# Relu² attention with an expert layer behind it: the high part of the routed rows made by ScalarE, and z split on one half of the partitions

## The chip, the cores and the metric

The kernel runs on one core of a Trainium2 chip. The metric is the device time of one execution in microseconds (us); the time shown for a kernel is the median of its runs. The five engines are TensorE (PE, with its weight loads shown apart as PEld), VectorE (DVE), ScalarE (ACT), GpSimd (POOL) and SyncE (SP), which here only issues DMAs.

## The reference

```python
def _attn_ref(u, v, z):                      # u, v: 8 x 2496 x 256, z: 8 x 2496 x 64
    scores = (1.0 / S) * np.matmul(z, z.transpose(0, 2, 1))
    attn = np.maximum(scores, 0.0) ** 2
    return u * np.matmul(attn, v)

def _moe_ref(x, expert_emb, tau, w1, w2):    # x: 19968 x 256, 8 experts, F = 1024
    xn, en = x / (norm(x) + 1e-6), expert_emb / (norm(expert_emb) + 1e-6)
    logits = xn @ en.T / tau
    expert_idx = np.argmax(logits, axis=1)
    gate_w = softmax(logits)[np.arange(N), expert_idx]
    for e in range(E):
        mask = expert_idx == e
        out[mask] = gate_w[mask, None] * (np.maximum(x[mask] @ w1[e], 0.0) @ w2[e])
```

The attention's output, 8 × 2496 rows, is the x of the expert layer. All is float32.

## The kernel before, in words

Every float32 operand of a large matmul is split into two float16 parts, a high part (the rounded value, scaled by a power of two) and a low part (the scaled value minus the high part), and a product is made of three or two float16 matmuls. So most splits are a pair of instructions: one that writes the high part and one that reads it back and subtracts.

**Attention.** Each of the 8 batches is worked in five groups g of 512 queries (the last has 448) by 20 tiles s of 128 keys, 100 steps per batch. `scores` (lines 257, 258) makes scores of one step in PSUM, ScalarE makes the relu and the square (`a`, lines 260, 261), and `parts` (lines 281, 282) makes the high and low part of it on VectorE (`hl`, or `joint` for the halved tiles on the diagonal). As the scores are symmetric, only steps with s // 4 >= g, the own steps, are computed; the others use tiles that DMA transposes have turned (`tt`, line 288). Scores run three own steps ahead. `values` (lines 320, 322, 324) multiplies by v into `acc`.

**z.** For the scores a batch needs two tiles of 128 partitions by 2560 columns: `z1` has the high part on partitions 0 to 63 and the low part on 64 to 127, `z2` the other way round. `z_load` (line 172) loads z twice, on both halves of the partitions, 256 columns at a time, into one of three buffers `zt`, and `z_split` (lines 183 to 186) makes the four parts, high ones on ScalarE (183, 184), low ones on VectorE (185, 186). The ten pieces of the next batch are split at steps 68, 70, ... 86 of the batch before; its first scores are made at step 97.

**v.** `v_load` (line 192) and `v_split` (229 on ScalarE, 230 on VectorE) run some steps ahead in the same way, in buffers `vt` and `vv`.

**Routing.** When a group ends, its 512 rows are routed by a queue of small functions, of which each step of the next group takes one: `gate_x` (352, multiplies acc by u into `xt`), `turn` (358, 359, matmuls that transpose and make the logits), `take` (369, ScalarE copies them to `x`), `square` (365, ScalarE), `root` and `scale` (608 to 622 and 378 to 387 on VectorE, which make the scale `up` and the logits), `top` (406 to 418, up to the one-hot `ob`), `exps` (424), four `split`s (395 the high, 396 the low part of 128 rows, into `row`), `gates`, `rank` (441, matmuls on `ob` that count), `place`, and `scatters` (465, GpSimd writes the rows to memory, sorted by expert).

**Weights of the experts** are split in the same time: `maxes` (504) and `scales` (510, 512), and four parts each (555 ScalarE, 556 VectorE, into `wo`), of which every second is followed by a 1 MB store to `wsd` (559).

**Expert layer.** From 1328 us on, PE runs the experts' matmuls (lines 869 to 895); the matmuls are nearly alone there.

**Order.** The order of PE's instructions is that of the program (a manual schedule). That of VectorE, ScalarE, GpSimd and SP is chosen by a scheduler at build time; each engine then takes its instructions strictly in that order. Dependencies are kept by regions of a tile.

Of the kernel before, what the change touches and what calls it, by code (L numbers as in the profile page):

```python
# [13 lines left out]
AF = mybir.ActivationFunctionType  # L14
ALU = mybir.AluOpType
# [4 lines left out]
P = 128  # L20
# [11 lines left out]
def ceil_div(a, b):  # L32
    return -(-a // b)
# [11 lines left out]
def relu2_attention_then_moe(ctx, tc, zT, uT, v, emb, tau, w1, w2, ident, tri, iota_e, out):  # L45
    nc = tc.nc
    B, D, S = uT.shape
    DQ = zT.shape[1] // 2
# [6 lines left out]
    SP = NST * P  # L55
# [34 lines left out]
    Zs = {}  # L90
# [9 lines left out]
    def scan_load(b, what, i, eng=None):  # L100

        t = wk.tile([P, SCAN], F32, name="scan", tag="scan", bufs=2)
        if what == "z":
            src = zT[b, i * (DQ // ZSCANS):(i + 1) * (DQ // ZSCANS), :]
        else:
            src = v[b, i * (SP // VSCANS):(i + 1) * (SP // VSCANS), :]
        (eng or nc.sync).dma_start(t, src.rearrange("a c -> (a c)").rearrange("(p w) -> p w", p=P))
        scan[b, what, i] = t

    def scan_max(b, what, i):  # L110
        if i == 0:
            n = ZSCANS if what == "z" else VSCANS if b else NV0
            scan[b, what] = sml.tile([P, n], F32, name="smx" + what)
        nc.vector.tensor_reduce(scan[b, what][:, i:i + 1], scan.pop((b, what, i)), axis=AX.X, op=ALU.max,
                                apply_absolute_value=True)
# [47 lines left out]
    def z_tiles(b):  # L163
        Zs[b] = (zpool.tile([P, SP], F16, name="z1", tag="z1"),
                 zpool.tile([P, SP], F16, name="z2", tag="z2"))

    ZC = 256

    def z_load(b, c0):
        zt = zpool.tile([P, ZC], F32, name="zt", tag="zt", bufs=3)  # L170
        c1 = min(c0 + ZC, SP)
        nc.sync.dma_start(zt[:, :c1 - c0], zT[b, :, c0:c1])
        zraw[b, c0] = zt

    def z_split(b, c0):
        zt = zraw.pop((b, c0))
        w = min(ZC, SP - c0)
        c1 = c0 + w
        z1, z2 = Zs[b]
        c = slice(c0, c1)  # L180
        lo, hi = slice(0, DQ), slice(DQ, P)
        k = scan[b, "cz"]
        nc.scalar.activation(z1[lo, c], zt[lo, :w], AF.Copy, scale=k[lo])
        nc.scalar.activation(z2[hi, c], zt[hi, :w], AF.Copy, scale=k[hi])
        nc.vector.scalar_tensor_tensor(z2[lo, c], zt[lo, :w], k[lo], z1[lo, c], op0=ALU.mult, op1=ALU.subtract)
        nc.vector.scalar_tensor_tensor(z1[hi, c], zt[hi, :w], k[hi], z2[hi, c], op0=ALU.mult, op1=ALU.subtract)  # L186

    vraw = {}

# [142 lines left out]
    def route(b, g, acc, ut):  # L332
# [8 lines left out]
        xk = x.rearrange("p j (k c) -> p j k c", k=2)[:, :, :, 0:P]  # L341
# [49 lines left out]
        def split(j):  # L391
            up = loc["up"][:, j:j + 1]
            hi = row16[:, j, 0:D].rearrange("p (k c) -> p k c", k=2)
            lo = row16[:, j, D:2 * D].rearrange("p (k c) -> p k c", k=2)
            nc.vector.tensor_scalar_mul(hi, xk[:, j], up)
            nc.vector.scalar_tensor_tensor(lo, xk[:, j], up, hi, op0=ALU.mult, op1=ALU.subtract)

        def splits(j0):
            def f():
                for j in range(j0, min(j0 + 2, nj)):  # L400
                    split(j)
            return f
# [173 lines left out]
    ZN = ceil_div(SP, ZC)  # L576
    for k in range(2):
        z_load(0, k * ZC)
    for i in range(NV0):
        v_first(i)  # L580
    z_load(0, 2 * ZC)
    for what, i in SCANS[:ZSCANS]:
        scan_max(0, what, i)
    for f in scale_pieces(0, "z"):
        f()
    for k in range(2):
        z_split(0, k * ZC)
# [5 lines left out]
    for i in range(NV0):  # L593
        scan_max(0, "v", i)
        if i == NV0 - 2:
            halves[direct[0]] = parts(*direct[0], probs.pop(direct[0]))
    z_load(0, 3 * ZC)
    for f in scale_pieces(0, "v"):
        f()
# [339 lines left out]
    def ahead(b):  # L939

        todo = []
        at = min(NST + 4, NB // 4)
        for i, what in enumerate(SCANS):
            todo.append((at + 2 * i, False, lambda w=what: scan_load(b + 1, *w)))
            todo.append((at + 2 * i + 4, False, lambda w=what: scan_max(b + 1, *w)))
        at += 2 * len(SCANS) + 4
        for k, what in enumerate("zv"):
            for j, f in enumerate(scale_pieces(b + 1, what)):
                todo.append((at + 8 * k + 4 * j, True, f))
        at = max(at + 20, (NG - 2) * NST // 2) if NG > 2 else at + 20  # L950
        gap = max(1, (NB - early - at) // ZN)
        todo.append((0, False, lambda: z_tiles(b + 1)))
        for k in range(ZN):
            todo.append((max(0, at + (k - 3) * gap), False, lambda k=k: z_load(b + 1, k * ZC)))
            todo.append((at + k * gap, False, lambda k=k: z_split(b + 1, k * ZC)))
        return sorted(todo, key=lambda x: x[0])

    todo = []
    nd = 0
    for i, (b, g, q, s) in enumerate(steps):  # L960
        own = s // GT >= g
        if i % 2 == 0 and zk < ZN:
            if zk + 2 < ZN:
                z_load(0, (zk + 2) * ZC)
            z_split(0, zk * ZC)
            zk += 1
# [3 lines left out]
        if q == 0:  # L970
            accs[b, g] = [psA.tile([P, 512], F32, name=f"acc{k}", tag=f"a{2 * ((b * NG + g) % 2) + k}") for k in range(2)]
            nx = (b, g + 1) if g + 1 < NG else (b + 1, 0)
            if nx[0] < B:
                uts[nx] = u_load(*nx)
            if g == 0 and b + 1 < B:
                todo = ahead(b)
# [34 lines left out]
        if b + 1 < B:  # L1011
            if (g == NG - 2 and q >= NST - early) or (NG > 1 and g == NG - 1) or NG == 1:
                k = q - (NST - early) if g == NG - 2 else q + early
# [128 lines left out]
```

## Time and profile before

| | |
|---|---|
| median of 3 runs | 2179.89 us (2178.35 to 2180.82) |
| profiled execution | 2175.33 us, span 2173.6 us |
| granted TensorE clock in it | 0.999 |
| PE busy | 2127.6 us, 98% |
| DVE busy | 1370.5 us, 63% |
| ACT busy | 1063.2 us, 49% |
| POOL busy | 337.9 us, 16% |
| DMA | 313.85 MB, 144 GB/s on average |

Busy times are shares of the span, an average over stages: DVE and ACT work mostly in the first 1300 us, PE throughout. In rows of the timeline the columns are the start, the duration, engine, line, operation, `out<-in`, shapes, count, and in brackets the idle time of the engine before it with what ended it. In rows of groups they are count, busy time, mean ns of one, and the idle time before. In rows of waits they are the total, the number and the longest.

### The profile page before, as it was taken

What the parts mean: (1) busy time and instruction counts of PE and PEld (TensorE: products, weight loads), DVE (VectorE), ACT (ScalarE), POOL (GpSimd) and SP (SyncE); (2) the same over time, 40 slices, a digit from 0 to 9 for tenths busy, and PEclk for the clock granted to TensorE, in tenths of its full rate; (3) what the DMA queues carried; (4) which work ended last, traced back from release to release, by engine and by line L of the source; (5) the groups of instructions that cost most, each with busy time, mean ns of one, the idle gap of its engine ahead of it and who ended that gap; (6) DMA issues with size and microseconds to landing.
All of it is one profiled execution on the core that took longest, in us unless ns stands there. A gap on an engine that the chain in (4) does not pass through costs nothing. (4 is left out here: it accounts for less than half of the span.)

```text
span 2173.6 us, 41442 instructions
## 1 busy us (share of the span) xinstructions
PE 2127.6 (98%) x14634; PEld 1406.9 (65%) x14634; DVE 1370.5 (63%) x4051; ACT 1063.2 (49%) x2193; POOL 337.9 (16%) x428
## 2 busy tenths in 40 slices
PE   6999999999999999999999999999999999999999
PEld 2445445545455545445545447888888888888898
DVE  7788788778788888788778664433333333333333
ACT  7567567667658667567667552222222222222211
POOL 0011111111111111111111111221111211111111
PEclk9999999999999999999999999999999999999999
DMA  7958767876867958767856852434323332246484
GB/s 199 210 106 223 168 159 186 183 180 148 204 156 179 224 112 221 170 156 186 186 129 136 174 95 91 136 72 96 86 53 89 91 94 52 50 122 191 128 219 116
DMA packets 554964, 313.85 MB, mean 144 GB/s; under 512 B 474741, under 2 KB 517118, under 8 KB 546560
## 3 DMA queue, kind: packets, MB, share of 16 engines
q1 hardware_dynamic: 539280, 269.53, 54.2%
q0 software_dynamic: 15184, 41.24, 5.9%
q8 instruction: 117, 1.92, 0.4%
q14 instruction: 95, 0.78, 0.1%
q10 hardware_dynamic: 288, 0.39, 0.1%
HBM read 277.53 MB, written 59.60 MB: 155 GB/s over the span
## 5 line engine op out<-in xcount | busy, mean ns | idle before, releaser
L260 ACT ACTIVATE a<-sc 128x512 f32<-128x512 f32 (+1 forms) x480 | 269.4, 561 | 168.2 <-PE sc L258 115.5
L261 ACT ACTIVATE a<-a 128x512 f32<-128x512 f32 (+1 forms) x480 | 286.8, 597 | 13.0
L324 PEld LDWEIGHTS <-vv 128*128 128x128 f16 x1600 | 156.7, 98 | 185.9 <-issue 8.2
L320 PEld LDWEIGHTS <-vv 128*128 128x128 f16 x1600 | 156.5, 98 | 159.8 <-ACT vv L229 1.1
L900 POOL DMA_INDIRECT out_dram<-ot,me x159 | 154.7, 973 | 653.5 <-DVE ot L899 629.3
L322 PEld LDWEIGHTS <-vv 128*128 128x128 f16 x1520 | 148.8, 98 | 163.1 <-issue 11.8
L895 PE MATMUL po<-w,hl 128*128 128x256 f16 x928 | 252.9, 273 | 0.0
L893 PE MATMUL po<-w,hh 128*128 128x256 f16 x928 | 252.9, 273 | 0.0
L894 PE MATMUL po<-w,hh 128*128 128x256 f16 x928 | 252.9, 273 | 0.0
L320 PE MATMUL acc<-tt,vv 128*128 128x512 f16 (+1 forms) x640 | 235.9, 369 | 0.0
L322 PE MATMUL acc<-tt,vv 128*128 128x512 f16 (+1 forms) x640 | 235.8, 368 | 0.0
L465 POOL DMA_INDIRECT xs<-row,dsti x160 | 166.0, 1038 | 391.0 <-DMA xs<-row,dsti 336.0
L899 DVE TENSOR_SCALAR ot<-po,me,w 128x256 f32<-128x256 f32 x116 | 58.3, 540 | 220.3 <-PE po L895 219.0
L324 PE MATMUL acc<-tt,vv 128*128 128x512 f16 (+1 forms) x640 | 183.5, 368 | 0.0
L257 PE MATMUL sc<-z 128*128 128x512 f16 (+1 forms) x480 | 175.7, 366 | 3.7 <-DVE z L186 3.1
L258 PE MATMUL sc<-z,z 128*128 128x512 f16 (+1 forms) x480 | 175.7, 366 | 0.0
L894 PEld LDWEIGHTS <-hh 128*128 128x128 f16 x1272 | 124.5, 98 | 15.1 <-issue 0.9
L895 PEld LDWEIGHTS <-hl 128*128 128x128 f16 x1272 | 124.5, 98 | 14.4
L893 PEld LDWEIGHTS <-hh 128*128 128x128 f16 x1272 | 124.5, 98 | 14.3
L369 ACT COPY x<-pt 128x264 f32<-128x264 f32 x160 | 59.6, 372 | 129.3 <-PE pt L359 126.5
L893 PE MATMUL po<-wb,hh 128*128 128x256 f16 x344 | 93.8, 273 | 0.8 <-DMA wb<-wsd 0.8
L895 PE MATMUL po<-wb,hl 128*128 128x256 f16 x344 | 93.8, 273 | 0.0
(3881 smaller groups left out, 4980.1 us busy)
## 6 DMA issues: line engine op xcount, KB each, us to landing
w<-wsd SPq DMA_DIRECT2D x64, 1026.0 KB
wa<-wsd SPq DMA_DIRECT2D x46, 1024.0 KB
w<-wsd SPq DMA_DIRECT2D x42, 1024.0 KB
wb<-wsd SPq DMA_DIRECT2D x24, 1026.0 KB
vt<-in_v_dram SPq DMA_DIRECT2D x140, 128.0 KB
scan<-in_v_dram SPq DMA_DIRECT2D x56, 320.0 KB
ut<-in_uT_dram SPq DMA_DIRECT2D x32, 512.0 KB
wr<-in_w_dram SPq DMA_DIRECT2D x16, 1024.0 KB
```

The costliest lines, as they stand in the source:

```text
L257: nc.tensor.matmul(sc[:, :n], z1[:, ss], z1[:, t0:t0 + n], start=True, stop=False)
L258: nc.tensor.matmul(sc[:, :n], z1[:, ss], z2[:, t0:t0 + n], start=False, stop=True)
L260: state["at"] = nc.scalar.activation(a[:, :n], sc[:, :n], AF.Relu, scale=2.0 ** -SHIFT).ins
L261: nc.scalar.activation(a[:, :n], a[:, :n], AF.Square)
L320: nc.tensor.matmul(o, va, ph, start=first, stop=False)
L322: nc.tensor.matmul(o, vb, ph, start=False, stop=False)
L324: nc.tensor.matmul(o, vb if last else va, pl, start=False, stop=ends)
L465: put = nc.gpsimd.indirect_dma_start(xs[:, :], bass.IndirectOffsetOnAxis(ap=loc["dsti"][:m, j:j + 1], axis=0), row[:m, j, :], None)
L893: nc.tensor.matmul(o, hh[:, f, t], wh, start=(f == 0), stop=False)
L894: nc.tensor.matmul(o, hh[:, f, t], wl, start=False, stop=False)
L895: nc.tensor.matmul(o, hl[:, f, t], wh, start=False, stop=(f == NF - 1))
L900: put = nc.gpsimd.indirect_dma_start(out, bass.IndirectOffsetOnAxis(ap=me.bitcast(U32)[:, j, 1:2], axis=0), ot[:, j, :], None, bounds_chec ...
```

## The change

There are two parts. In `split` the high part of a routed row is made by ScalarE's Copy with scale `up` in place of VectorE's multiplication; the low part stays on VectorE and reads it. And for every batch but the first, z is loaded on 64 partitions only and split there (two instructions for a piece in place of four); after pieces 5 and 9 a new function `z_copy` copies the columns that are ready to the other 64 partitions by two DMAs each, the low part of `z2` to `z1` and the high part of `z1` to `z2`. Lines behind the change are moved on by 9 (260 to 269, 281 to 290, 365 to 374, 369 to 378, 395 to 404, 396 to 405, 418 to 427, 441 to 450, 555 to 564, 608 to 617).

```diff
     def z_load(b, c0):
         ...
-        nc.sync.dma_start(zt[:, :c1 - c0], zT[b, :, c0:c1])
+        m = P if b == 0 else DQ
+        nc.sync.dma_start(zt[:m, :c1 - c0], zT[b, :m, c0:c1])
     def z_split(b, c0):
         ...
         nc.scalar.activation(z1[lo, c], zt[lo, :w], AF.Copy, scale=k[lo])
-        nc.scalar.activation(z2[hi, c], zt[hi, :w], AF.Copy, scale=k[hi])
+        if b == 0:
+            nc.scalar.activation(z2[hi, c], zt[hi, :w], AF.Copy, scale=k[hi])
         nc.vector.scalar_tensor_tensor(z2[lo, c], zt[lo, :w], k[lo], z1[lo, c], op0=ALU.mult, op1=ALU.subtract)
-        nc.vector.scalar_tensor_tensor(z1[hi, c], zt[hi, :w], k[hi], z2[hi, c], op0=ALU.mult, op1=ALU.subtract)
+        if b == 0:
+            nc.vector.scalar_tensor_tensor(z1[hi, c], zt[hi, :w], k[hi], z2[hi, c], op0=ALU.mult, op1=ALU.subtract)
+
+    def z_copy(b, c0, c1):
+        z1, z2 = Zs[b]
+        c = slice(c0, c1)
+        nc.sync.dma_start(z1[DQ:P, c], z2[0:DQ, c])
+        nc.sync.dma_start(z2[DQ:P, c], z1[0:DQ, c])
     ...
         def split(j):
             ...
-            nc.vector.tensor_scalar_mul(hi, xk[:, j], up)
+            nc.scalar.activation(hi, xk[:, j], AF.Copy, scale=up)
             nc.vector.scalar_tensor_tensor(lo, xk[:, j], up, hi, op0=ALU.mult, op1=ALU.subtract)
     ...
         for k in range(ZN):
             todo.append((max(0, at + (k - 3) * gap), False, lambda k=k: z_load(b + 1, k * ZC)))
             todo.append((at + k * gap, False, lambda k=k: z_split(b + 1, k * ZC)))
+            if k in (ZN // 2, ZN - 1):
+                c0, c1 = (0, (k + 1) * ZC) if k == ZN // 2 else ((ZN // 2 + 1) * ZC, SP)
+                todo.append((at + k * gap, False, lambda c0=c0, c1=c1: z_copy(b + 1, c0, c1)))
```

The order of PE's instructions is the same before and after. That of the others shifts. On VectorE, at the beginning of the routing of batch 1's group 0 (`xn2c` to `up` belong to root and scale, `xt2` and `xy` to the square root, `hl` to own steps), before:

```order
L381 TENSOR_SCALAR up_2973<-h23_2971 128x4
L383 TENSOR_SCALAR dn_2975<-h23_2971 128x4
L615 TENSOR_TENSOR xt_2934<-xy_2932 128x4
L395 TENSOR_SCALAR row_2779<-x_2776,up_2973 128x256
L617 SCALAR_TENSOR_TENSOR xt2_2936<-xt_2934,xn2c_2928 128x4
L395 TENSOR_SCALAR row_2779<-x_2776,up_2973 128x256
L281 CAST hl__2908<-a_2876 128x4x128
L114 TENSOR_REDUCE smxz_2918<-scan_2835 128x1
L282 TENSOR_TENSOR hl__2908<-a_2876,hl__2908 128x4x128
```

and after:

```order
L390 TENSOR_SCALAR up_2957<-h23_2955 128x4
L392 TENSOR_SCALAR dn_2959<-h23_2955 128x4
L624 TENSOR_TENSOR xt_2918<-xy_2916 128x4
L626 SCALAR_TENSOR_TENSOR xt2_2920<-xt_2918,xn2c_2912 128x4
L628 SCALAR_TENSOR_TENSOR xy_2922<-xt2_2920,xy_2916 128x4
L443 TENSOR_SCALAR row_3201<-iot_222 128x4
L624 TENSOR_TENSOR xt_2924<-xy_2922 128x4
L290 CAST hl__2892<-a_2860 128x4x128
L114 TENSOR_REDUCE smxz_2902<-scan_2819 128x1
L291 TENSOR_TENSOR hl__2892<-a_2860,hl__2892 128x4x128
```

The two high parts ahead of the cast are gone, and pieces of the square root have moved up.

On ScalarE, at the routing of batch 0's group 3, beside splits of v and the last parts of an expert's weights (`pt` is what the matmuls of `turn` write), before:

```order
L369 COPY x_1952<-pt_2049 128x264
L365 ACTIVATE sq_2085,n2_1954<-x_1952 128x256
L229 ACTIVATE vv_2069<-vt_1999,scv_1561 128x256
L369 COPY x_1952<-pt_2065 128x264
L365 ACTIVATE sq_2098,n2_1954<-x_1952 128x256
L555 ACTIVATE wo_2180<-wr2_818,wup_1649 128x512
L229 ACTIVATE vv_2087<-vt_2023,scv_1561 128x256
L555 ACTIVATE wo_2180<-wr2_818,wup_1649 128x512
```

and after:

```order
L378 COPY x_1942<-pt_2033 128x264
L374 ACTIVATE sq_2069,n2_1944<-x_1942 128x256
L564 ACTIVATE wo_2164<-wr2_818,wup_1649 128x512
L238 ACTIVATE vv_2053<-vt_1987,scv_1561 128x256
L378 COPY x_1942<-pt_2049 128x264
L564 ACTIVATE wo_2164<-wr2_818,wup_1649 128x512
L374 ACTIVATE sq_2082,n2_1944<-x_1942 128x256
L238 ACTIVATE vv_2071<-vt_2009,scv_1561 128x256
L564 ACTIVATE wo_2164<-wr2_818,wup_1649 128x512
L238 ACTIVATE vv_2084<-vt_2023,scv_1561 128x256
L404 ACTIVATE row_1945<-x_1942,up_2134 128x256 x2
```

Two parts of the weights now stand ahead of the last square, and the high parts of the rows follow behind it.

On SP, near the end of batch 1 (`zt` and `vt` are loads for batch 2, `ut` for the next group, `wr2` a weight load), before:

```order
L559 DMA wsd_73<-wo_3818 128x4096
L172 DMA zt_3997<-in_zT_dram 128x256
L496 DMA wr2_4162<-in_w2_dram 128x8x256
L329 DMA ut_4042<-in_uT_dram 128x2x512
L172 DMA zt_4053<-in_zT_dram 128x256
L192 DMA vt_4097<-in_v_dram 128x256
```

and after:

```order
L568 DMA wsd_73<-wo_3798 128x4096
L194 DMA z1_2338<-z2_2339 64x1536
L195 DMA z2_2339<-z1_2338 64x1536
L173 DMA zt_3971<-in_zT_dram 64x256
L338 DMA ut_4016<-in_uT_dram 128x2x512
L173 DMA zt_4025<-in_zT_dram 64x256
L201 DMA vt_4067<-in_v_dram 128x256
```

The first pair of copies stands ahead of the last loads of zt; the second pair comes eight loads later.

## The prediction

> **What bounds the kernel.** I read the totals of the page first, then the time by stages, then what TensorE waits for, and last the timeline around each of these waits.
>
> ```profile
> PE 2127.6 (98%) x14634; PEld 1406.9 (65%) x14634; DVE 1370.5 (63%) x4051; ACT 1063.2 (49%) x2193; POOL 337.9 (16%) x428
> ```
>
> TensorE (PE) is busy for 2127.6 of 2173.6 us. A change that takes no matmul away can win at most the other 46 us, and only those parts that the touched engines cause. The stages, as window and its length, then PE, weight loads, DVE, ACT and POOL busy, the granted clock, the DMA share and GB/s:
>
> ```profile
> 60.00:1220.00 1160.00, 1145.13 (x5871) 581.98 (x5870) 949.23 (x3118) 779.96 (x1674) 160.53 (x230) 1.00 0.73 172
> 1290.00:2173.00 883.00, 876.00 (x8276) 774.83 (x8274) 332.51 (x659) 206.97 (x363) 167.50 (x175) 1.00 0.42 105
> ```
>
> Attention and routing fill the first window: PE is idle there for 1160 − 1145.13 = 14.9 us, DVE is busy 82% and ACT 67% of the time. In the second window DVE works 38% and ACT 23%; what the change does after 1290 us (17 of the 160 high parts) lies beside matmuls and is costed at nothing; at worst, if all 17 stood on the path, it would be 17 × 0.4 = 7 us. The waits of PE from 60 to 1220 us (total, times, longest):
>
> ```profile
> PE pm L441 <- DVE ob L418: 4.7, 3, 1.7
> PE pt L358 <- DVE xt L352: 2.3, 2, 1.5
> PE acc L320 <- DVE hl__5470 L281: 1.9, 1, 1.9
> PE pm L512 <- DVE mx L510: 1.3, 2, 1.0
> PE acc L320 <- DVE hl__7183 L281: 0.9, 1, 0.9
> PE acc L320 <- DVE hl__11329 L281: 0.4, 1, 0.4
> PE acc L320 <- DVE hl__3015 L281: 0.4, 1, 0.4
> PE acc L324 <- DVE hl__5470 L282: 0.4, 1, 0.4
> PE acc L324 <- DVE hl__13784 L282: 0.4, 1, 0.4
> PE acc L320 <- DVE hl__13784 L281: 0.3, 1, 0.3
> PE acc L324 <- DVE hl__7075 L282: 0.3, 1, 0.3
> PE acc L324 <- DVE hl__7148 L282: 0.3, 1, 0.3
> PE acc L320 <- DVE hl__7272 L281: 0.2, 1, 0.2
> ```
>
> Their sum is 13.8 us, and every releaser is DVE. So the change works on the right engine, but the pot is 13.8 us, 0.6% of the time.
>
> **The change, part by part.** The prices, by shape:
>
> ```profile
> L396 DVE SCALAR_TENSOR_TENSOR row<-x,up,row 128x256 f16<-128x256 f32 x160 | 76.0, 476 | 0.0
> L395 DVE TENSOR_SCALAR row<-x,up 128x256 f16<-128x256 f32 x160 | 54.9, 347 | 0.0
> L186 DVE SCALAR_TENSOR_TENSOR z<-zt,scz,z 64x256 f16<-64x256 f32 x80 | 38.8, 485 | 3.2
> L184 ACT ACTIVATE z<-zt,scz 64x256 f16<-64x256 f32 x80 | 40.2, 503 | 1.7
> L229 ACT ACTIVATE vv<-vt,scv 128x256 f16<-128x256 f32 x133 | 63.0, 500 | 16.1 <-PE acc L324 8.2 <-DVE scv L142 4.3 <-DMA vt<-in_v_dram 2.6
> ...
> 180.06 1.69 ACT L229 ACTIVATE vv<-vt,scv 128x256 f16<-128x256 f32 x4
> 441.00 0.34 DVE L395 TENSOR_SCALAR row<-x,up 128x256 f16<-128x256 f32 x1
> 441.26 0.15 DVE L617 SCALAR_TENSOR_TENSOR xt<-xt,xn2c 128x4 f32<-128x4 f32 x1
> ```
>
> Instructions of one engine overlap a little, so what one takes from its neighbours is the distance between starts: on DVE a high part takes 441.26 − 441.00 = 0.26 us. On ACT its nearest row is the split of v, the same shape and function: four in 1.69 us, (1.69 − 0.50) / 3 = 0.40 us each. DVE is freed of 160 × 0.26 = 41.6 us and of 70 halves of z at 0.485, 34 us. ACT gains 160 × 0.40 = 64 us and loses 70 × 0.50 = 35 us, in net +29 us, to 70% of the first window. All this lies beside PE; it counts only at the waits above, so I go through them.
>
> *Routing beside own steps* (first excerpt of the order). In batch 1's routing of group 0 the wait is this:
>
> ```profile
> 248.97 0.41 DVE L281 CAST hl__3015<-a 128x512 f16<-128x512 f32 x1
> 249.43 0.38 PE L320 MATMUL acc<-hl__3015,vv 128*128 128x512 f16 x1 [0.44 <-DVE hl__3015 L281]
> ```
>
> DVE runs its queue back to back here, and four high parts stood ahead in the same route, 4 × 0.26 = 1.05 us. That is more than the 0.44 us of the wait, so it goes. The same holds for hl__11329 (0.4) and for the two waits on mx behind them (1.3): −2.1 us. For hl__7075, 7148, 7183 and 7272 (1.7 together, one place) a saving of 1.05 is all that is ahead: −1.05. Next late there is the same cast, by the 0.65 left.
>
> *The three waits of rank on ob* (4.7): in each the four high parts stand on DVE between root and ob, so I take −1.05 of each, −3.1. Against it stands that ACT is now longer just there (second excerpt of the order):
>
> ```profile
> 169.94 0.34 SPq L559 DMA_DIRECT2D wsd<-wo  x1
> 174.45 0.17 DVE L608 TENSOR_SCALAR xn2c<-n 128x4 f32<-128x4 f32 x1
> 176.79 0.72 ACT L555 ACTIVATE wo<-wr,wup 128x512 f16<-128x512 f32 x1 [2.38 <-DMA wsd<-wo]
> ```
>
> The weight split (L555, after L564) waits until the store of the piece before has landed, 176.79. It now stands ahead of the last take and square, on which root (174.45) rests. Taken at these times root would be 176.79 + 0.72 + 0.4 + 0.6 − 174.45 = up to 4 us later; but the store too may be earlier, since wo's pieces have less of ACT and DVE before them. Bounds for the three together: −4.7 to +6 (two of the three places have this order). I stay at −3.1, since behind root there are fewer splits of v than before.
>
> *hl__5470* (1.9 + 0.4) stands behind high parts too, the one at 441.00 above:
>
> ```profile
> 443.74 0.41 DVE L281 CAST hl__5470<-a 128x512 f16<-128x512 f32 x1
> ```
>
> But there three of the four now lie on ACT ahead of the next relu, so that its operand comes later by about what DVE gains: 0, bounds −1.05 and +1. *xt* (2.3) is not behind any high part in this route, *hl__13784* (0.7) neither: 0, with −0.7 as the gain if freed DVE time reaches them.
>
> *What is moved on ACT.* The high parts wait for `up`, and the relu of an own step stands behind them. In group 0's routes:
>
> ```profile
> 238.97 0.19 ACT L365 ACTIVATION_READ_ACCUMULATOR sq<-x 128x1 f32 x1
> 239.06 0.58 ACT L260 ACTIVATE a<-sc 128x512 f32<-128x512 f32 x1
> 239.70 0.16 DVE L381 TENSOR_SCALAR up<-h 128x4 int32<-128x4 int32 x1
> 240.51 0.42 DVE L281 CAST hl__2908<-a 128x512 f16<-128x512 f32 x1
> 243.65 0.38 PE L320 MATMUL acc<-hl__2908,vv 128*128 128x512 f16 x1
> ```
>
> The relu at 239.06 now comes behind `up` (239.86) and one high part, at 240.26: 1.2 us later; the next, behind a second one, 1.5 us later. Its cast ended at 240.93 and PE needed it at 243.65, so 2.7 us lay between. The shift is hidden with 1.2 us to spare: 0. If that cover goes, each such place costs what is beyond 2.7 (rival 3). The low part on DVE now waits for ACT; behind it in DVE's queue stand own casts with the same 2.7 us: 0.
>
> *z* (third excerpt). The two copies stand on SP behind the split of piece 5 and of piece 9. In batch 1:
>
> ```profile
> 327.38 0.48 DVE L186 SCALAR_TENSOR_TENSOR z<-zt,scz,z 64x256 f16<-64x256 f32 x1
> 337.82 0.48 DVE L186 SCALAR_TENSOR_TENSOR z<-zt,scz,z 64x256 f16<-64x256 f32 x1
> 349.42 0.38 PE L257 MATMUL sc<-z 128*128 128x512 f16 x1
> ```
>
> Piece 5 is done at 327.86 and the next batch's first score starts at 349.42: 21.6 us for the first copy (64 × 3072 B, twice). The second (twice 64 × 2048 B) feeds only the keys from 1536 on, twelve scores later. The trace has no transfer within SBUF; the nearest row is the 1 MB store above, which landed within 176.79 − 169.94 = 6.85 us, five times the bytes of a copy. The four issues on SP per batch (0.34 us each by the store's row) push the loads of zt and vt behind them back by 1.4 us; no wait of PE above names a DMA, so that is costed at 0, at most 7 × 1.4 = 10 us if SP were on the path. Half loads of z (64 partitions) take no more than whole ones did. Without cover, a copy of L us would cost 7 × (L − 21.6).
>
> **Sum**: −2.1 − 1.05 − 3.1 = −6.2, and I take 0.8 back for the later root of the second place, −5.4 us. The profiled execution took 2175.33 us (span 2173.6), 4.6 below the median of the three runs, 2179.89; on that median the forecast is 2174.5 us. The bounds add up to −2.1 − 1.7 − 4.7 − 1.05 − 0.7 = −10 and −2.1 − 1.05 + 6 = +3, so its own range is 2170 to 2183.
>
> One rule speaks against the change. The Trainium skill, "Perfetto Trace Analysis", section "Optimizing Scalar/DVE Operations", says that an operation which both engines can do is faster on DVE where DVE has a performance mode for it, and that giving it to ScalarE may make sense if DVE is saturated. The rows agree on the first half (347 against 500 ns). DVE at 82% is not saturated over the stage, so by that rule the moved parts would bring nothing and the time would be that of rival 2.
>
> **The rivals.** (1) *All DVE waits of the stage go.* If DVE is freed of 76 us in 1160 (6.5%) it may be ahead everywhere: −13.8 us, 2166.1 us. For it: every releaser above is DVE. Against it: xt and hl__5470 do not stand behind what is removed. (2) *The waits are swapped.* The low part waits for ACT, ACT for `up`, root for the later square; what DVE wins it spends waiting: 0 ± 3, 2179.9 us. For it: 4.7 us of the pot lies where the weight split moved ahead. (3) *ACT holds its queue.* The high parts wait for `up` with relus behind them at the 24 routes that run beside own steps (groups 0, 1 and 4 of eight batches). It decides when `up` comes more than 1.2 us later than in the rows above, 0.89 us after the square began its last read; if at all 24 the relu is 0.8 us beyond its cover, 24 × 0.8 = +19, less 5.4: about 2193 us. Against it: in the row above `up` needs no wait for DVE, and DVE becomes emptier. Late copies come to about the same time at L = 23.5 (7 × 1.9 = +13), more than three times the store's 6.85 us.
>
> **How the numbers follow.** Forecast 0.46, rival 1 0.14, rival 2 0.25, rival 3 0.11, late copies 0.04. 0.2% is 4.4 us, about what a measurement of this kernel can tell. Faster by more: two thirds of the forecast (0.31), rival 1 (0.14) and nothing else, 0.45. Slower: rival 3, the copies and a little of rival 2, 0.17. The rest, 0.38, is within. For 8 in 10 the range reaches over rivals 1 and 2 with their spread and leaves rival 3's far end out: 2165 to 2186.
>
> **What would show it.** In the profile after, DVE's busy time should be about 54.9 + 34 = 89 us lower, ACT's 160 × 0.5 − 35 = 45 us higher. In the waits of PE, hl at 249 us and mx at 261 should be gone, rank's three be near 0.5 us each, xt's unchanged. No wait of PE should name a DMA into z, nor ACT's a. It is wrong if rank's waits grow (the weight split ahead of the take), if casts beside routes wait for ACT's a and PE for them, or if the first score of a batch waits for a copy.

## The result, and the profile after

The changed kernel takes 2208.59 us (median of 4 runs, 2205.68 to 2211.75) against 2179.12 us before: a ratio of 1.014, 95% interval 1.0117 to 1.0163. It is slower by some 30 us, where 5 us less were forecast and at most 2186 us were held likely. The totals of the page:

```profile
PE 2141.8 (97%) x14634; PEld 1409.9 (64%) x14634; DVE 1313.1 (60%) x3821; ACT 1080.1 (49%) x2283; POOL 346.0 (16%) x428
```

and the window of attention and routing (columns as above):

```profile
60.00:1220.00 1160.00, 1128.46 (x5718) 569.62 (x5717) 873.05 (x2825) 770.99 (x1704) 165.11 (x225) 0.99 0.72 168
```

VectorE (DVE) is relieved, by 57 us of busy time, and TensorE (PE) waits more all the same: it is idle for 1160 − 1128.46 = 31.5 us of the window in place of 14.9. Over the whole span PE is idle for 2203.8 − 2141.8 = 62.0 us in place of 46.0, and it is busy 14.2 us longer for the same 14634 matmuls; the two, 16.0 and 14.2, make up the 30.2 us by which the spans differ. The largest waits of PE in the window from 60 to 1220 us:

```profile
PE pm L450 <- DVE ob L427: 13.5, 4, 4.9
PE pt L367 <- DVE xt L361: 6.2, 6, 1.9
PE acc L329 <- DVE hl__7500 L290: 3.5, 1, 3.5
PE acc L329 <- DVE hl__5438 L290: 1.6, 1, 1.6
```

Rank (4.7 us before) and xt (2.3) wait more, and a new wait of 3.5 us has come. All of them still name VectorE, so the next question is what VectorE waits for. Its own waits from 60 to 1330 us, of the kernel before:

```profile
DVE xn2c L608 <- ACT sq L365: 64.4, 20, 8.4
...
DVE row L434 <- DMA xs<-row,dsti: 2.9, 2, 1.6
```

and of the changed kernel, from 60 to 1350 us:

```profile
DVE xn2c L617 <- ACT sq L374: 76.5, 21, 8.4
DVE row L443 <- DMA xs<-row,dsti: 50.3, 16, 8.0
```

Line 443 (434 before) is one small instruction in `gates` that writes the row numbers into `row`, 0.17 us long. It waited 2.9 us in all, and now waits 50.3 us, for scatters that still read the row buffer. One such place in the timeline is near the end of batch 1, where the routing of group 3 runs:

```profile
338.32 0.96 POOL L474 DMA_INDIRECT xs<-row,dsti  x1 [3.84 <-DMA xs<-row,dsti]
344.29 0.16 DVE L390 TENSOR_SCALAR up<-h 128x4 int32<-128x4 int32 x1
344.62 0.16 DVE L626 SCALAR_TENSOR_TENSOR xt<-xt,xn2c 128x4 f32<-128x4 f32 x1
345.31 0.96 POOL L474 DMA_INDIRECT xs<-row,dsti  x1 [6.04 <-DMA xs<-row,dsti]
350.79 0.17 DVE L443 TENSOR_SCALAR row<-iot 128x4 int32<-128x4 f32 x1 [6.01 <-DMA xs<-row,dsti]
351.37 0.48 DVE L405 SCALAR_TENSOR_TENSOR row<-x,up,row 128x256 f16<-128x256 f32 x1
357.05 0.27 PE L450 MATMUL pm<-ob,ones_b 128*128 128x40 bf16 x4 [3.99 <-DVE ob L427]
357.90 0.58 PE L329 MATMUL acc<-hl__3984,vv 128*128 128x448 f16 x1
```

In the middle of the square root that leads to `ob`, VectorE stops for 6.01 us at a row-number write. It is not the write of this route: it belongs to the *next* one, whose row buffer (there are two) is that of the route before, and that route's last scatter was only issued at 345.31. Rank then waits 3.99 us, and the matmuls behind it take 0.58 us in place of 0.35 for a while. So this wait of PE is paid twice, as idle time and as slower matmuls behind it. The other three waits of rank and the new one of hl__7500 look the same: three to seven us ahead of each, VectorE ends a stop at the row numbers, of 3.87, 1.89, 8.00 and 6.65 us. The longest is

```profile
1021.39 0.17 DVE L443 TENSOR_SCALAR row<-iot 128x4 int32<-128x4 f32 x1 [8.00 <-DMA xs<-row,dsti]
```

with rank's wait of 4.88 us behind it.

The order had it in view. The excerpt of VectorE above shows `L443 TENSOR_SCALAR row_3201<-iot_222` behind `xy_2922`, in the middle of a route's square root, although `row_3201` is the buffer of the next route. In the whole program, the next group's row numbers stand ahead of the last low part of the running route in 35 of 39 routes; in the kernel before it was 2 of 39, and in the median they stood 4 rows behind that low part. The scheduler moves them up once the high parts are not on VectorE.

### The profile page after: what moved, and what is told of

Same layout as the page of the kernel before. It is cut to its first block, busy times and chain, and to the rows that moved or that the text cites. A ratio compares the mean times of both kernels' runs of the same rounds, so it can differ in the third digit from the quotient of the medians.

```text
span 2203.8 us, 41437 instructions
## 1 busy us (share of the span) xinstructions
PE 2141.8 (97%) x14634; PEld 1409.9 (64%) x14634; DVE 1313.1 (60%) x3821; ACT 1080.1 (49%) x2283; POOL 346.0 (16%) x428
## 5 line engine op out<-in xcount | busy, mean ns | idle before, releaser
L474 POOL DMA_INDIRECT xs<-row,dsti x160 | 172.7, 1079 | 419.9 <-DMA xs<-row,dsti 361.9
L902 PEld LDWEIGHTS <-hh 128*128 128x128 f16 x1272 | 124.5, 98 | 14.2
```

The costliest lines, as they stand in the source:

```text
L474: put = nc.gpsimd.indirect_dma_start(xs[:, :], bass.IndirectOffsetOnAxis(ap=loc["dsti"][:m, j:j + 1], axis=0), row[:m, j, :], None)
L902: nc.tensor.matmul(o, hh[:, f, t], wh, start=(f == 0), stop=False)
```

## The experiments

Three theories were set against each other. Theory 1: the row numbers' write, moved ahead, holds VectorE until scatters land. Theory 2: ScalarE, with the high parts in its queue, holds the relus (the third rival of the prediction). Theory 3: the copies of z delay other transfers or the first scores.

**One part of the change alone.** In `z_only` the high parts stay on VectorE:

```diff
-            nc.scalar.activation(hi, xk[:, j], AF.Copy, scale=up)
+            nc.vector.tensor_scalar_mul(hi, xk[:, j], up)
```

> The high parts of the routed rows stay on VectorE; only the half split of z and its copies are made. Theory 1 (the write of the row numbers, line 443, was moved ahead on VectorE and waits there for scatters): its place is the old one here, so that wait stays at 3 us or less and the time is 2172 to 2180 us, as 34 us of VectorE fall away. Theory 2 (ScalarE is held by the high parts): no high parts there, 2172 to 2180 us too. Theory 3 (the copies delay other transfers or the first scores): 2195 us or more.

Measured: 2172.22 us against 2176.12, 0.9978 (0.9969 to 0.9987). The row numbers stand where they stood (ahead in 2 of 39 routes), with these waits:

```profile
DVE row L443 <- DMA xs<-row,dsti: 3.2, 2, 2.3
DVE row L443 <- POOL vv L236: 2.7, 1, 2.7
```

Theory 3 falls: the copies cost nothing, and the half split is a gain of 0.2%.

`hi_only` is the kernel before with only the high parts on ScalarE, the diff above the other way round.

> Only the high parts move to ScalarE; z is split on both halves as before. Theory 1: the row numbers' write again stands ahead of the low parts and VectorE waits there 40 us or more in all; 2200 to 2215 us. Theory 2: 2200 to 2215 us as well, but with VectorE waiting for the relu and squares of ScalarE and not at the row numbers. Theory 3: 2175 to 2182 us.

Measured: 2190.54 us, 1.0068 (1.0053 to 1.0084). That is half of the whole change's loss, and 10 us under what theory 1 gave. The order is the one of theory 1 (32 of 39 routes), but the wait is shorter than the 40 us expected:

```profile
DVE row L434 <- DMA xs<-row,dsti: 27.5, 14, 4.1
```

and the timeline at the place shown above is

```profile
337.11 0.96 POOL L465 DMA_INDIRECT xs<-row,dsti  x1 [5.05 <-DMA xs<-row,dsti]
340.73 0.17 DVE L434 TENSOR_SCALAR row<-iot 128x4 int32<-128x4 f32 x1
```

The last scatter is issued at 337.11 here, and at 340.73 the write finds its buffer free. In the full change that scatter came at 345.31, 8 us later. Earlier waits of the same kind delay a route's rows and so its scatters, for which the next write waits; in the full change the two pairs of copies are also issued near this place. Which of the two makes up the other half was not separated.

**The write put back.** In `after_late` the changed kernel stays whole, but the row numbers may be issued only behind the last low part of their own route:

```diff
-            nc.vector.scalar_tensor_tensor(lo, xk[:, j], up, hi, op0=ALU.mult, op1=ALU.subtract)
+            loc["lo"] = nc.vector.scalar_tensor_tensor(lo, xk[:, j], up, hi, op0=ALU.mult, op1=ALU.subtract).ins
...
-            nc.vector.tensor_scalar_add(rowi[:, :nj, D + 1:D + 2], idb[:, :nj].unsqueeze(2), float(b * S + t0))
+            with tc.issue_after(loc["lo"]):
+                nc.vector.tensor_scalar_add(rowi[:, :nj, D + 1:D + 2], idb[:, :nj].unsqueeze(2), float(b * S + t0))
```

> The changed kernel in full, with the write of the row numbers pinned behind the last low part of its own route. Theory 1: the 50 us of VectorE's wait for scatters vanish, rank waits 5 us or less in all, and the time is 2168 to 2180 us. Theory 2 and theory 3: nothing is gained, 2200 us or more.

Measured: 2174.75 us, 0.9993 (0.9984 to 1.0002). The loss is gone, as theory 1 has it, and PE's waits for rank are gone entirely. What is left as its largest wait is xt:

```profile
PE pt L367 <- DVE xt L361: 8.3, 8, 1.7
```

**The write alone, moved.** `early` is the kernel before, without either part of the change. Only the row numbers of the next group are written right behind `dn` of this one:

```diff
+                nxt = rt.tile([P, 4, ROW], F32, name="row", tag="row")
+                with tc.issue_after(behind_dn):
+                    nc.vector.tensor_scalar_add(nxt.bitcast(I32)[:, :, D + 1:D + 2], idb[:, :].unsqueeze(2), float(b1 * S + groups[g1][0]))
+                state["row"] = nxt
```

> The kernel before, high parts on VectorE and z as it was, with only the row numbers of the next group written right behind dn in the route of this group. Theory 1: this alone makes VectorE wait 40 us or more for scatters and costs 15 to 45 us, 2195 to 2225 us. Theories 2 and 3: 2175 to 2183 us.

Measured: 2204.72 us, 1.0123 (1.0101 to 1.0144), nearly the whole loss of the change without the change. VectorE's wait at the write (line 397 here), and the page's totals:

```profile
DVE row L397 <- DMA xs<-row,dsti: 41.7, 21, 6.3
```

```profile
PE 2140.5 (97%) x14634; PEld 1408.9 (64%) x14634; DVE 1372.1 (62%) x4051; ACT 1060.1 (48%) x2193; POOL 337.9 (15%) x428
```

PE's busy time, 2140.5 us, rises here as it did with the change. So the place of this one write is sufficient for the loss; theory 2 gave no change.

**The parts with the write pinned.** `hi_late` and `z_late` are `hi_only` and `z_only` with the pin of `after_late`.

> Only the high parts on ScalarE, z as before, and the row numbers pinned behind the last low part. Theory 1 (the row numbers' place is the whole loss): no wait of VectorE for scatters at the row numbers, 2172 to 2180 us, so the 0.7% of the high parts alone is gone. If the high parts also cost something by themselves on ScalarE (what is left of theory 2), 2181 to 2188 us.

> Only the half split of z with its copies, high parts on VectorE, row numbers pinned. Theory 1: with the two waits at the row numbers (3.2 and 2.7 us on VectorE) gone too it is 2169 to 2173 us, at or below the half split of z alone. Theory 2 expects the same. If the place of the row numbers does not matter where it does not wait, no change against it within 2 us.

Measured: `hi_late` 2180.29 us, 1.0018 (1.0007 to 1.0029); `z_late` 2170.72 us, 0.9983 (0.9970 to 0.9995). The half split keeps its gain. The high parts alone still cost 0.2% with this pin, and the trace puts it on xt:

```profile
PE pt L358 <- DVE xt L352: 8.3, 7, 2.4
```

against 2.3 us before. `after_late_scan` and `z_late_scan` tried a reason for that, since in seven of the eight places of `after_late` VectorE waits for a scan's load just ahead of xt (one line: each maximum of a scan is taken at `at + 2 * i + 6` in place of `+ 4`).

> The changed kernel with the row numbers pinned, and each maximum of a scan taken two steps later, six steps behind its load. What is left with the pin are eight waits of TensorE for xt, 8.3 us, at group 1's ends, where VectorE waits for a scan load first. Theory 1 with the waits handed on to the scan loads: these waits fall to 3 us or less and the time to 2165 to 2171 us. If VectorE's waits for scans do not matter: 2172 to 2178 us.

> As the one before, but with the high parts on VectorE. If the scans matter: 2166 to 2171 us. If the high parts on ScalarE are a gain once nothing waits behind the row numbers, this is 2 to 5 us slower than the same with them on ScalarE; if they cost, 2 to 5 us faster.

Measured: 2172.31 and 2172.67 us, 0.9988 (0.9977 to 0.9998) and 0.9990 (0.9980 to 1.0000), both within 0.1% of the same kernels without it, and no different from each other. PE's waits of `after_late_scan` (those for xt fell, others came):

```profile
PE pt L367 <- DVE xt L361: 4.7, 4, 1.8
PE acc L329 <- DVE hl__15416 L290: 2.0, 1, 2.0
PE pm L522 <- DVE mx L520: 1.2, 2, 0.7
```

VectorE's waits for scans, of `after_late` and then of `after_late_scan`:

```profile
DVE smxv L114 <- DMA scan<-in_v_dram: 27.2, 13, 5.0
```

```profile
DVE smxv L114 <- DMA scan<-in_v_dram: 39.5, 21, 4.7
```

The expectation of 2165 to 2171 us failed. The edit did not take the suspect away, though: VectorE waits longer for scans than without it, so the run does not clear them. The timelines tell more. At the end of group 1 of batch 1 the kernel before has xt ahead of the next maximum:

```profile
264.13 0.67 DVE L352 TENSOR_TENSOR xt<-acc,ut 128x512 f32<-128x512 f32 x1
264.73 1.52 DVE L114 TENSOR_REDUCE smxv<-scan 128x1 f32<-128x640 f32 x2
```

and `after_late` has one maximum more ahead of xt, which waits for its load:

```profile
261.78 0.82 DVE L114 TENSOR_REDUCE smxv<-scan 128x1 f32<-128x640 f32 x1 [2.25 <-DMA scan<-in_v_dram]
263.30 1.27 DVE L361 TENSOR_TENSOR xt<-acc,ut 128x512 f32<-128x512 f32 x2
264.03 0.50 PE L367 MATMUL pt<-rhs,xt 128*128 128x136 f32 x2 [1.42 <-DVE xt L361]
```

Counted in VectorE's order, one maximum more than in the kernel before stands ahead of xt at this point in five of the six batches 1 to 6, in `hi_only`, `hi_late`, `after_late`, the changed kernel and `after_buf3` alike; in `z_only` and `z_buf3` the counts are those of the kernel before. So, with the high parts on ScalarE, it was moved up into the gap like the row numbers. In `after_late_scan` it is back behind xt in four of the five. That these waits are all of the 0.2% is not shown, as xt's waits fell there and the time hardly did.

**The wait taken away, the order kept.** A third row buffer leaves the write where the change put it (35 of 39 routes) and frees what it waits for. The room comes from u:

```diff
-        ut = rt.tile([P, 2, 512], F32, name="ut", tag="ut")
+        ut = rt.tile([P, 2, 512], F32, name="ut", tag="ut", bufs=1)
-        row = rt.tile([P, 4, ROW], F32, name="row", tag="row")
+        row = rt.tile([P, 4, ROW], F32, name="row", tag="row", bufs=3)
-            if nx[0] < B:
-                uts[nx] = u_load(*nx)
+        if q == 2 and (b, g) not in uts:
+            uts[b, g] = u_load(b, g)
```

> The changed kernel with three buffers for the routed rows in place of two; the room comes from u, which has one buffer in place of two and is loaded in its own group. The write of the row numbers stands as far ahead on VectorE as in the changed kernel, but its buffer is that of three routes before, whose scatters have long landed. Theory 1: the wait there falls from 50 us to 3 or less and the time to 2170 to 2181 us. If it is the place of the write or the new order as such, or ScalarE (theory 2): 2200 us or more.

> The changed kernel with u's single buffer alone and two buffers for the rows, as a control: every theory expects 2200 to 2215 us, and the wait at the row numbers as in the changed kernel (40 us or more). If it is 2185 us or less, the buffer of u and not that of the rows is what the run with three buffers shows.

Measured: `after_buf3` 2169.06 us, 0.9964 (0.9951 to 0.9977); the control `after_ut1` 2195.18 us, 1.0093 (1.0073 to 1.0113). No wait of VectorE for scatters at the row numbers is left in the first; in the control it stands as in the change, and PE waits for rank:

```profile
DVE row L443 <- DMA xs<-row,dsti: 47.3, 18, 6.1
```

```profile
PE pm L450 <- DVE ob L427: 7.2, 4, 3.0
```

The control is 5 us under the range expected for it; with u's single buffer rank waits 7.2 us in place of 13.5, though the wait on VectorE is nearly the same, and why was not looked into. The step from two to three buffers is worth 1.3%, and with it the change has the lowest median of all that ran. So the loss comes neither from the write's place alone nor from ScalarE, but from the place together with a buffer that is not free.

**What the change is worth without the wait.** The last two put the same buffers under the kernel before and under `z_only`.

> The kernel before with three buffers for the rows and one for u. It measures what the change itself is worth once nothing waits at the row numbers. If the change then brings the 5 us that were forecast, this is 2172 to 2177 us against the 2169 of the changed kernel with the same buffers; if it brings nothing, 2167 to 2171 us.

> The same buffers, z split on one half and copied, high parts on VectorE. If the high parts on ScalarE cost something by themselves, as they did with the pinned write (1.0018 for them alone), this is 2164 to 2168 us, faster than both together; if they are a gain once the row buffer is free, 2170 to 2174 us.

Measured: `before_buf3` 2181.39 us, 1.0023 (1.0009 to 1.0036); `z_buf3` 2171.37 us, 0.9976 (0.9966 to 0.9986). `before_buf3` is slower than both of its expectations: these buffers cost the kernel before 0.23%, and every version with u's single buffer has a wait of PE of 2.2 us at 50 us that the kernel before has not. Against `before_buf3` the half split is worth 0.47% and the whole change 0.59%, some 12 to 13 us; against the kernel before as it was, the change with three buffers is worth 0.36%. `z_buf3` lies in the range expected if the high parts are a gain, but between it and `after_buf3` (0.12%) the intervals overlap, so the sign of the high parts alone is not settled there. PE's waits for rank with these buffers, of the kernel before, and of the half split:

```profile
PE pm L441 <- DVE ob L418: 4.9, 3, 2.2
```

```profile
PE pm L450 <- DVE ob L427: 1.2, 2, 1.0
```

In the whole change none is left; its largest wait there, and its totals, with PE's busy time back at 2126.1 us:

```profile
PE pt L367 <- DVE xt L361: 3.4, 6, 1.3
```

```profile
PE 2126.1 (98%) x14634; PEld 1406.9 (65%) x14634; DVE 1317.2 (61%) x3821; ACT 1083.2 (50%) x2283; POOL 346.8 (16%) x428
```

## Why the prediction was wrong

**The step that failed** is the first one of the change's part, "Routing beside own steps", and with it the three waits of rank: VectorE's queue was taken as the one before with four instructions cut out. What else the scheduler puts into the gap was not read, though the quoted excerpt held it. The term left out is a wait of VectorE of 50.3 us for scatters at the row numbers. It is behind most of the 16.0 us of added idle time of PE and the 14.2 us by which its matmuls took longer; `early` shows that the place of this write is enough for such a loss, `after_late` and `after_buf3` that hardly any of it remains without the wait.

**The gain came in part, and not from where it was forecast.** With the buffer free, rank's waits go to none (−3.1 of 4.7 was forecast) and those on mx go too. But two casts whose waits were to shrink or vanish, hl__7183 (0.9 us before) and hl__3015 (0.4), keep them in `after_buf3`, under other numbers:

```profile
PE acc L329 <- DVE hl__7133 L290: 1.0, 1, 1.0
PE acc L329 <- DVE hl__2997 L290: 0.6, 1, 0.6
```

The prediction took all of its gain from the high parts and costed the half split at nothing. In the runs the half split brings 0.17 to 0.47% by itself (`z_late`; `z_buf3` against `before_buf3`), and the high parts, with the wait at the row numbers gone, lie between a loss of 0.18% (`hi_late`) and a gain of 0.12% (`after_buf3` against `z_buf3`). That the whole, 0.36% against the kernel before with the row buffer free, is near the forecast 0.25% is luck.

**Rank and the weight split.** The bound of +6 us for the weight split ahead of the last square was not needed. At batch 0's group 3 root starts at

```profile
175.24 0.20 DVE L617 TENSOR_SCALAR xn2c<-n 128x4 f32<-128x4 f32 x1
```

0.8 us later than the 174.45 of before, not 4. Rank's wait behind it, 3.33 us in place of 1.66, comes after the stop of 3.87 us at the row numbers. In `after_late` no wait for rank is left.

**xt** was forecast unchanged at 2.3 us and waits 6.2 us in the change, 8.3 in `after_late`. The step that failed is the same: a scan's maximum was moved up ahead of it. How much of the time it costs stays open.

**ScalarE's queue** (rival 3) had the right side, with the wrong mechanism: no wait of PE between 60 and 1220 us names ScalarE. The price was right:

```profile
344.54 0.91 ACT L404 ACTIVATE row<-x,up 128x256 f16<-128x256 f32 x2 [0.37 <-issue]
```

Two high parts in 0.91 us, about 0.4 apart. The busy times were mis-sized: VectorE fell by 57 us and not 89, ScalarE rose by 17 and not 45, since the forecast summed whole durations of instructions, which overlap; the summed durations did fall by 90 and rise by 43 us. And of the high parts 8 lie after 1290 us, not 17 (17 lie after 1220); nothing hung on it.

**The copies** were hidden as said. The first is issued at 332.71, its reader starts at 360.14, and no wait of PE between 60 and 1220 us names a DMA:

```profile
332.71 0.48 SPq L194 DMA_DIRECT2D z<-z  x1
360.14 0.62 PE L266 MATMUL sc<-z 128*128 128x512 f16 x1
```

**The rule of the Trainium skill** that was weighed ("Perfetto Trace Analysis", "Optimizing Scalar/DVE Operations") gave no gain for the moved parts. The runs bear it out for the high parts with the pinned write (`hi_late`, 1.0018); with three buffers 0.12% the other way lies within the intervals.

## What to carry to other kernels

When an instruction leaves an in-order queue that a scheduler fills, read the new order for what has moved up into the gap, and for each such instruction ask which buffer it writes and who still reads it. Here it was a write that depends on nothing but a free buffer, and a maximum that depends on nothing but a load. Once moved up, each holds everything behind it on its engine until a transfer has landed; for the write, a pin or one more buffer took that away. Take a reason apart from both sides: one version that has only the suspect, one that has everything but the suspect.

## What the hardware showed

The cost of a wait of PE can be more than its length. Behind the four waits of 3.3 to 4.9 us in the changed kernel the granted clock over 4 us was 0.50 to 0.63; behind the one of 3.99 us it was 0.57:

```profile
357.00:361.00 4.00, 3.95 (x16) 1.70 (x17) 3.75 (x13) 2.55 (x6) 0.48 (x2) 0.57 0.45 128
```

The matmuls stayed slow for some 3 to 5 us after each. Set against the same matmuls in the trace of before, those behind the four waits took 8.8 us longer in all. The slow matmuls also came behind shorter waits, here from 1.7 us after the end of one of 1.85 us, which adds some 2 us:

```profile
775.54 0.50 PE L367 MATMUL pt<-rhs,xt 128*128 128x136 f32 x2 [1.85 <-DVE xt L361]
...
777.20 0.63 PE L331 MATMUL acc<-tt,vv 128*128 128x512 f16 x1
```

Together that is some 11 of the 14.2 us of longer busy time; the rest is spread over the trace. Waits of 1.3 to 1.6 us in the same trace left no slow matmul. In the fourteen traces of this case, from 40 us on, the granted clock was halved behind all 12 waits of PE of more than 3 us, behind none of the 15 from 1.3 to 1.67 us, and behind 22 of the 37 between. The Trainium skill, "TensorE: Matmul & The Clock Gate", section "What's actually happening", lets the clock fall to half after an idle window of about 3.4 us that runs freely. The halved speed agrees: in the slow stretch matmuls of this shape start 0.43 us apart, at full clock 0.22. But the window by itself does not explain a fall behind a wait of 1.85 us.
